# The first two weight blocks of an RWKV-5 and SwiGLU kernel, loaded and rounded by column halves

## The chip, the cores and the metric

The kernel runs on one core of one Trainium2 chip. The metric is the device time of one execution in microseconds (us); lower is better. A core has five engines that run programs of their own and meet at semaphores: TensorE (PE in the profile; its weight loads are PEld), VectorE (DVE), ScalarE (ACT), GpSimd (POOL) and SyncE (SP), which issues most of the DMAs. Sixteen DMA engines move what any of them issues.

## The reference

An RWKV-5 attention block with 4 batches, 8 heads, 768 steps and head size 48, in float32, feeds a SwiGLU feed-forward block of 3072 tokens, 384 channels and 1536 hidden channels:

```python
for t in range(S):
    kt, vt, rt = (k[:, :, t], v[:, :, t], r[:, :, t])
    cur = np.einsum('bhd,bhe->bhde', u[None] * kt, vt)
    y[:, :, t] = np.einsum('bhd,bhde->bhe', rt, state + cur)
    state = w[None, :, :, None] * state + np.einsum('bhd,bhe->bhde', kt, vt)
...
g = x @ w_gate
silu = g * (1.0 / (1.0 + np.exp(-g)))
val = x @ w_val
return (silu * val @ w_out).astype(np.float32)
```

Here x is y with its heads side by side, one row for each token. The three weight matrices arrive as float64 and r, k, v, w, u as float32.

## The kernel before

The attention is cut into 24 units of 128 steps; unit i is piece i // 4 of batch i % 4, up to unit 11. For one unit, `load(i)` fetches k and r (two DMAs on SP, rows of 48 floats), `load_v(i)` fetches v (two DMAs), `own_begin` and `own_end` form r*k*u on POOL, `own_sum` sums it on DVE, `diagonal` writes it into the tile At (ACT, and POOL for a part in the first units), `turn` transposes k and r on PE (line 405, eight matmuls, the four of k first) and DVE scales the results (line 407), `scores` multiplies them on PE (494) and DVE copies them under a mask into At (502), `outputs` multiplies At with v on PE (645) and ACT copies the result into xT (649), and `update` carries the state on (658). The raw k and r of units 0 to 3 are loaded into slots of the tile `hats`; r of unit 2 goes where r of unit 0 was.

The feed-forward block runs between these steps. `gate_value(g, f)` (line 688) multiplies 128 hidden columns f of w_gate and then of w_val with the x of units 2g and 2g+1, six float32 matmuls, each in two passes, so twelve in the profile; ACT applies Silu (694), DVE multiplies (695). `feed` takes such pieces out of a list at places that are fixed by hand.

The weights come as 64-bit floats, which no engine computes with, so they are rounded to float32 from their two 32-bit words. They are cut into 18 blocks (`chunks`); blocks 0 and 1 are the first 256 columns of w_gate and of w_val, 128 partitions times three rows of 256 doubles each. For a block, `load_weights` issues one DMA into a tile `bits` (three such tiles turn round; line 184), `round_high` turns the high words of one half into scaled magnitudes on ACT (204), `round_low` scales all the low words on ACT (210), `round_dve` puts sign and bits of one half into the weight tile on DVE (219 and 220), and `add_low` (228, one half) or `round_pool` (252, a whole block) adds the rounded low words on POOL. A half here is the first or the last 128 of the 256 columns, which are interleaved in the tile.

Every engine executes its instructions in the order in which the Python program issues them; nothing is reordered. On SP the order of the first loads is k and r of unit 0, k and r of unit 1, block 0, v of unit 0, block 1, v of unit 1, then k and r of unit 2, k and r of unit 3, block 2, v of units 2 and 3, block 3. On POOL, `own_begin(2)`, which reads k and r of unit 2, stands ahead of `add_low(0, 0)` and `add_low(1, 0)`; behind them come `own_end(2)`, `add_low(0, 1)`, `own_begin(3)`, `add_low(1, 1)`. The first `gate_value` needs `add_low(0, 0)` and, half way, `add_low(1, 0)`, and the x of units 0 and 1. The second needs the second halves. Between the two, PE transposes k and r of unit 3 and makes the scores of unit 2.

From unit 4 on the same steps run in a loop in which more blocks are rounded and more pieces fed; the later part multiplies by 3x3 schemes with fewer products (lines 957 and 1190) and projects with w_out (768).

Of the kernel before, what the change touches and what calls it, by code (L numbers as in the profile page):

```python
# [10 lines left out]
INT32 = mybir.dt.int32  # L11
UINT32 = mybir.dt.uint32
AF = mybir.ActivationFunctionType
ALU = mybir.AluOpType
AX = mybir.AxisListType
P = 128
# [6 lines left out]
def fast(  # L23
# [37 lines left out]
    two = ctx.enter_context(tc.tile_pool(name="two", bufs=2))  # L61
    three = ctx.enter_context(tc.tile_pool(name="three", bufs=3))
    ps_a = ctx.enter_context(tc.tile_pool(name="ps_a", bufs=1, space=bass.MemoryType.PSUM))
    ps_f = ctx.enter_context(tc.tile_pool(name="ps_f", bufs=1, space=bass.MemoryType.PSUM))
    dve, pool, act, pe, sp = nc.vector, nc.gpsimd, nc.scalar, nc.tensor, nc.sync
# [28 lines left out]
    def next_psum(m, n):  # L94
        t = ring_a[0]
        ring_a.rotate(-1)
        return t[:, 0 : m * n].rearrange("p (a x) -> p a x", a=m)
# [22 lines left out]
    def rhat_of(i):  # L120
        return rhat[i % 2 if i < BLOCKS else i % 4 // 2]

    def raw(i):

        if i < 4:
            return khat[i][:, :, 0:D], rhat[i % 2][:, :, 0:D]
        return k_ld[i % 2][:], r_ld[i % 2][:]
# [8 lines left out]
    def pieces_of(i):  # L136

        if i < PAIRED:
            c, b = divmod(i, B)
            return [(slice(0, P), b, P * c)]  # L140
        return [(slice(64 * p, 64 * p + 64), *part(i, p)) for p in range(2)]

    def load(i):
        for src, dst in zip((k, r), raw(i)):
            for rows, b, t in pieces_of(i):
                n = rows.stop - rows.start
                sp.dma_start(out=dst[rows], in_=src[b, :, t : t + n, :].rearrange("h t d -> t h d"))

    def load_v(i):
        for rows, b, t in pieces_of(i):  # L150
            n = rows.stop - rows.start
            for e in range(2):
                sp.dma_start(
                    out=v_ld[b][rows, :, 64 * e : 64 * e + D],
                    in_=v[b, :, t : t + n, :].rearrange("(a e) t d -> e t a d", e=2)[e],
                )


    chunks = []
# [9 lines left out]
    WN = 6 * P  # L169
    NW = len(chunks)  # L170
    bits, mags, lows = {}, {}, {}
    done = {"load": 0, "act": 0, "pool": 0}

    def next_chunk(stage):
        n = done[stage]
        done[stage] = min(n + 1, NW)
        return n if n < NW else None

    def load_weights():
        n = next_chunk("load")  # L180
        if n is not None:
            src = chunks[n][0].bitcast(INT32)
            bits[n] = three.tile([P, WN, 2], INT32, name="w_bits", tag="w_bits")
            sp.dma_start(
                out=bits[n][:].rearrange("p (c f) two -> p c (f two)", c=src.shape[1]), in_=src
            )
# [6 lines left out]
    def halves(x, n):  # L193

        c = chunks[n][1].shape[1]
        x = x.rearrange("p (c f) -> p c f", c=c)
        f = x.shape[2]
        return [x[:, :, 0 : f // 2], x[:, :, f // 2 : f]] if c == 3 else [x[:, 0:1], x[:, 1:2]]

    def round_high(n, half, bank):  # L200
        hi = halves(bits[n][:, :, 1], n)[half]
        mag = banks[2 + bank][:, 0 : WN // 2].bitcast(INT32)
        mags[n, half] = mag.rearrange("p (c f) -> p c f", c=hi.shape[1])
        act.activation(
            mags[n, half].bitcast(FP32), hi.bitcast(FP32), AF.Copy, scale=float(2.0**-112)
        )

    def round_low(n):
        lows[n] = two.tile([P, WN], INT32, name="w_low", tag="w_low")
        act.activation(  # L210
            lows[n][:], bits[n][:, :, 0].bitcast(UINT32), AF.Copy, scale=float(2.0**-29)
        )

    def round_dve(n, half):
        hi = mags.pop((n, half))
        f = hi.shape[2]
        dst = chunks[n][1].bitcast(INT32)
        dst = dst[:, :, half * f : half * f + f] if hi.shape[1] == 3 else dst[:, half : half + 1]
        dve.tensor_scalar(dst, hi, -(1 << 31), None, ALU.bitwise_and)
        dve.scalar_tensor_tensor(dst, hi, 3, dst, ALU.logical_shift_left, ALU.bitwise_or)  # L220

    def add_low(n, half):

        dst = chunks[n][1].bitcast(INT32)
        f = dst.shape[2] // 2
        cols = slice(half * f, half * f + f)
        low = lows[n][:].rearrange("p (c f) -> p c f", c=dst.shape[1])
        pool.tensor_tensor(dst[:, :, cols], dst[:, :, cols], low[:, :, cols], ALU.add)  # L228

    def round_first(n):  # L230
        round_high(n, 0, 0)
        round_low(n)
        round_dve(n, 0)

    def round_second(n):
        round_high(n, 1, 1)
        round_dve(n, 1)
        del bits[n]
        load_weights()
# [21 lines left out]
    def own_begin(i):  # L261
        kl, rl = raw(i)
        rks[i] = two.tile([P, H, D], FP32, name="rk", tag="rk")[:]
        pool.tensor_mul(rks[i], rl, kl)
# [8 lines left out]
    def own_sum(i):  # L273
        dus[i] = three.tile([P, H], FP32, name="du", tag="du")
        dve.tensor_reduce(dus[i][:], rks.pop(i), axis=AX.X, op=ALU.add)
# [12 lines left out]
    for e in range(2):  # L288
# [3 lines left out]
        out=u_row, in_=bass.AP(tensor=u.tensor, offset=u.offset, ap=[[0, 1], [1, H * D]]),  # L292
    )
    load(0)
    load(1)
    load_weights()
    load_v(0)
    load_weights()
    load_v(1)

    act.activation(sg0[:], ident[:, 0:1], AF.Silu)
    def warm(n, bank=None):
# [14 lines left out]
        out=mask[:, 0], in_=mask[:, 0], compare_op=ALU.is_gt, fill=0.0,  # L317
# [9 lines left out]
    for l in range(7):  # L327
        n = 1 << l
        f = pw[:, :, P - n : P - n + 1].to_broadcast([P, HP, n])
# [66 lines left out]
    def pair(t, a):  # L396
        return t[:, 2 * a : 2 * a + 2, :].rearrange("p e d -> p (e d)")

    def turn(i):
        kr = khat[i % 4], rhat_of(i)  # L400
        tps = [next_psum(HP, P) for _ in kr]
        turned[i] = three.tile([P, HP, P], FP32, name="rT", tag="rT")
        for tp, t, dst, table in zip(tps, kr, (kT[i % 2], turned[i]), (pw[:, :, 1 : P + 1], pv)):
            for a in range(HP):
                pe.transpose(tp[:, a, :], pair(t, a), ident[:])  # L405
            if i < 4:
                dve.tensor_mul(dst[:], tp[:], table)
            else:
                act.copy(dst[:], tp[:])
# [75 lines left out]
    def scores(i):  # L485

        ps = [next_psum(HP, P) for _ in range(2)]
        if i >= PAIRED:
            paired_scores(i, ps)
            return  # L490
        for a in range(HP):
            for e in range(2):
                rows = slice(64 * e, 64 * e + D)
                pe.matmul(  # L494
                    ps[e][:, a, :], kT[i % 2][rows, at(i, a), :], turned[i][rows, at(i, a), :],
                    start=True, stop=True, skip_group_check=True,
                )

        def masked_copy(e):
            dst = At[i % 2][:].rearrange("p (a e) t -> p a e t", e=2)[:, :, e]  # L500
            m = mask[:, 0].bitcast(INT32).unsqueeze(1).to_broadcast([P, HP, P])
            dve.copy_predicated(dst, m, ps[e][:])

        for e in range(2):
            lazy.append(lambda e=e: masked_copy(e))
        lazy.popleft()()
        if i < BLOCKS:
            lazy.popleft()()
# [854 lines left out]
    def flush():  # L1363
        while small:
            small.popleft()()
# [8 lines left out]
    diagonal(0)  # L1374
    flush()
    load(2)
    turn(1)
    own_sum(1)
    load(3)
# [4 lines left out]
    diagonal(1)  # L1384
    flush()
    round_high(0, 0, 0)
    round_low(0)
    round_high(1, 0, 1)
    round_low(1)
    scores(1)  # L1390
    round_dve(0, 0)
    own_begin(2)
# [11 lines left out]
    queue(0)  # L1404
    for n in range(2):
        round_high(n, 1, n)
        round_dve(n, 1)
        add_low(n, 1)
        del bits[n], lows[n]
        if n == 0:  # L1410
            own_sum(2)
            own_begin(3)
# [138 lines left out]
    n = nc.values_load(outside, min_val=0, max_val=512)  # L1551
# [6 lines left out]
@with_exitstack  # L1558
def kernel(
    ctx: ExitStack,  # L1560
    tc: tile.TileContext,
    *args: bass.AP,
):
    nc = tc.nc
    ctx.enter_context(tc.manual_schedule())
    flag = ctx.enter_context(tc.tile_pool(name="flag", bufs=1))
    outside = flag.tile([1, 1], INT32, name="outside")
    n = fast(tc, *args, outside[:])
    with tc.If(n > 0, label="general"):
        general(tc, *args)  # L1570
# [397 lines left out]
```

## Time and profile before

| | us |
|---|---|
| median of 3 runs | 581.36 |
| lowest and highest of them | 580.2 and 581.39 |
| the profiled execution, whole | 584.59 |
| its span, first to last instruction | 582.8 |
| busy in it: PE / DVE / POOL / ACT | 571.9 / 426.7 / 391.5 / 224.2 |

The profiled execution is one run of the program with the hardware profiler on; all rows below are from it, with times counted from the start of its span. The names in a row are the program's: "wgv<-wgv,w_low" writes tile wgv and reads wgv and w_low, "L228" is the line, "x2" the number of instructions, and what stands in brackets is the idle time before the group and what ended it. DMA rows on SP give the time of the issue, not that of the transfer.

### The profile page before, as it was taken

Reading aid. Unit: us, or ns where it says so; the run is one execution under the profiler, and the core shown is the slowest. Engines: PE = TensorE matmul, PEld = TensorE weight load, DVE = VectorE, ACT = ScalarE, POOL = GpSimd, SP = SyncE. Lnnn points to the kernel's source line nnn. Section 1 sums busy time; section 2 is a strip of 40 time slices with the busy share of each in tenths; the row PEclk is TensorE's granted clock in tenths of the full one; section 3 lists DMA queues with packets and bytes.
Section 4 is the critical chain, followed back from the end, with each engine's and each line's share of the span. In section 5 each row is a group of like instructions: output and inputs, shape, how many; then the busy total and the mean of one; then the engine's idle time right before and its main releaser. Section 6 shows DMA issues by size and latency. Waiting matters only on the chain.

```text
span 582.8 us, 13575 instructions
## 1 busy us (share of the span) xinstructions
PE 571.9 (98%) x5370; PEld 515.8 (89%) x5370; DVE 426.7 (73%) x745; ACT 224.2 (38%) x532; POOL 391.5 (67%) x395
## 2 busy tenths in 40 slices
PE   8899999999999999999999999999999999999996
PEld 7688888899988899988889988899988899988896
DVE  7677887488497789597869587869358877477672
ACT  3568878322354521344431343421143320233310
POOL 6589887999999737979536979527988950010610
PEclk9899999999999999999999999999999999999999
DMA  8978888562535425544324544220200000200002
GB/s 202 229 210 236 225 288 121 68 108 50 117 64 98 75 40 110 124 76 88 63 54 90 122 80 80 50 39 21 55 0 1 0 1 2 55 0 2 2 1 57
DMA packets 151734, 48.09 MB, mean 83 GB/s; under 512 B 139313, under 2 KB 142386, under 8 KB 151666
## 3 DMA queue, kind: packets, MB, share of 16 engines
q1 hardware_dynamic: 147218, 40.69, 33.9%
q10 hardware_dynamic: 4448, 6.49, 4.0%
q8 instruction: 43, 0.70, 0.5%
q14 instruction: 25, 0.20, 0.1%
HBM read 28.31 MB, written 4.72 MB: 57 GB/s over the span
## 4 chain that ended last, share of the span: by engine, by line
PE 97%; DMA 1%; issue 0%; DVE 0%; POOL 0%; ACT 0%; POOLq 0%
PE bank L957 32%; PE bank L768 19%; PE ring L957 13%; PE bank L688 12%; PE bank L1190 8%; PE ring L645 3%; PE ring L580 2%; PE ring L494 2%; PE ring L405 1%; PE ring L546 1%; PE ring L1190 1%; DMA hats<-in_r_dram 1%; PE ring L594 1%; PE ring L658 1%; PE ring L306 1%
## 5 line engine op out<-in xcount | busy, mean ns | idle before, releaser
L981 DVE TENSOR_TENSOR hv<-hv,bank 128x512 f32<-128x512 f32 x132 | 87.8, 682 | 38.5 <-PE bank L957 32.8
L688 PE MATMUL bank<-xT,wgv 128*128 128x256 f32 x288 | 68.3, 392 | 1.7 <-POOL wgv L228 1.5
L957 PE MATMUL bank<-xf,wgv 128*128 128x256 f32 x256 | 65.7, 381 | 0.0
L688 PEld LDWEIGHTS bank<-xT,wgv 128*128 128x128 f32 x288 | 54.3, 193 | 10.4 <-POOL wgv L228 1.7
L981 ACT COPY hv<-bank 128x512 f32<-128x512 f32 x72 | 40.8, 584 | 58.3 <-PE bank L957 52.7
L957 PEld LDWEIGHTS bank<-xf,wgv 128*128 128x128 f32 x256 | 48.0, 190 | 6.8 <-DVE kT L1235 0.6
L1244 POOL TENSOR_TENSOR hv<-At,hats 128x512 f32<-128x512 f32 x8 | 10.2, 1274 | 63.8 <-ACT At L1243 63.8
L988 ACT ACTIVATE hv<-hv 128x512 f32<-128x512 f32 (+2 forms) x36 | 22.7, 633 | 49.0 <-DVE hv L981 49.0
L376 ACT ACTIVATE zs<-mask,du 128x64 f32<-128x64 f32 x96 | 29.8, 346 | 20.4 <-DVE hv L781 9.3
L957 PE MATMUL bank<-xT,wgv 128*128 128x256 f32 x144 | 35.5, 379 | 0.0
L957 PE MATMUL bank<-xT,s 128*128 128x256 f32 x152 | 35.2, 380 | 0.0
L768 PE MATMUL bank<-wt,hs 128*128 128x192 f32 x192 | 34.1, 328 | 0.0
L768 PE MATMUL bank<-wo,hs 128*128 128x192 f32 x192 | 33.8, 326 | 0.0
L745 POOL TENSOR_TENSOR hs<-hv,hs 128x768 f32<-128x768 f32 x6 | 11.2, 1875 | 32.6 <-DVE hs L742 32.6
L768 PE MATMUL bank<-wo,hv 128*128 128x192 f32 x192 | 32.8, 327 | 0.0
L957 PEld LDWEIGHTS bank<-xT,s 128*128 128x128 f32 x152 | 28.7, 190 | 4.2 <-issue 0.2
L887 POOL TENSOR_TENSOR s<-s,wgv 128x256 f32<-128x256 f32 x39 | 30.1, 772 | 2.9
L768 PEld LDWEIGHTS bank<-wo,hv 128*128 128x128 f32 x192 | 31.6, 190 | 0.4
L887 POOL TENSOR_TENSOR s<-s 128x256 f32<-128x256 f32 x39 | 31.3, 802 | 0.9
L768 PEld LDWEIGHTS bank<-wo,hs 128*128 128x128 f32 x192 | 31.7, 190 | 0.2
L768 PEld LDWEIGHTS bank<-wt,hs 128*128 128x128 f32 x192 | 31.4, 190 | 0.2
L887 POOL TENSOR_TENSOR s<-wgv 128x256 f32<-128x256 f32 x39 | 29.6, 776 | 1.8 <-PE bank L768 1.8
(239 smaller groups left out, 1439.8 us busy)
## 6 DMA issues: line engine op xcount, KB each, us to landing
hats<-hats SPq DMA_DIRECT2D x96, 64.0 KB, 2.4
w_bits<-in_moe_w_gate_dram SPq DMA_DIRECT2D x6, 768.0 KB
w_bits<-in_moe_w_val_dram SPq DMA_DIRECT2D x6, 768.0 KB, 6.3
w_bits<-in_moe_w_out_dram SPq DMA_DIRECT2D x6, 768.0 KB, 7.0
At<-zs ACTq DMA_DIRECT2D x24, 128.0 KB, 3.7
At<-rT SPq DMA_DIRECT2D x24, 128.0 KB, 2.3
v_ld<-in_v_dram SPq DMA_DIRECT2D x24, 96.0 KB, 5.1
k_ld<-in_k_dram SPq DMA_DIRECT2D x24, 96.0 KB, 3.9
```

The source lines that it names most:

```text
L376: lambda h=h: act.activation(own[:, i % 2, slot(i, h), :], ident64, AF.Identity, scale=du[:, h : h + 1])
L494: pe.matmul(ps[e][:, a, :], kT[i % 2][rows, at(i, a), :], turned[i][rows, at(i, a), :], start=True, stop=True, skip_group_check=True,)
L580: pe.matmul(ps[32 * q : 32 * q + 32, cc, 64 * p : 64 * p + 64], *x, start=start, stop=stop, skip_group_check=True,)
L645: pe.matmul(ps[32 * q : 32 * q + 32, cc, :], *x, start=start, stop=stop, skip_group_check=True,)
L688: pe.matmul(gv[:, o, :].rearrange("p (i t) -> p i t", i=2), wt[:, c, P * f : P * (f + 1)], xT[:, 2 * g % NX : 2 * g % NX + 2, c, :], start ...
L745: on.tensor_sub(s[1], h12, x["s"][1])
L768: pe.matmul(ps, lhs[:, f, :], rhs[:, f, :], start=(f == 0 and n in (0, 1, 4)), stop=(f == FH - 1), skip_group_check=True,)
L887: op(made[o], made[a], made[b])
L957: pe.matmul(ps[:, o], u[:, o], v, start=first and o == 0, stop=True, skip_group_check=True,)
L981: do(out, *(pair_of(wide[a][:]) if isinstance(a, str) else a for a in args))
L988: todo.append((at, lambda: act.activation(gate, gate, AF.Silu)))
L1190: pe.matmul(ps, (h[what][q] if h[what] is D_ else h[what][:, q])[:, f, :], wide["o"][what][:, f, :], start=first and f == 0 and (split or ...
```

## The change

Blocks 0 and 1 are loaded by column halves. `load_half(n, half)` issues one DMA for 128 of the block's 256 columns; the first halves of both blocks are issued ahead of v of unit 0, where block 0 was, and the second halves behind k and r of unit 2, ahead of k and r of unit 3. `round_low` gets a half too: that of the first halves stays in its place, that of the second halves is done behind `round_high(n, 1, n)`. The later blocks are loaded and rounded whole, as before.

```diff
+    def load_half(n, half):
+
+        src = chunks[n][0].bitcast(INT32)
+        if half == 0:
+            bits[n] = three.tile([P, WN, 2], INT32, name="w_bits", tag="w_bits")
+            done["load"] = n + 1
+        c, f = src.shape[1], src.shape[2] // 2
+        sp.dma_start(
+            out=bits[n][:].rearrange("p (c f) two -> p c (f two)", c=c)[:, :, f * half : f * half + f],
+            in_=src[:, :, f * half : f * half + f],
+        )
+
...
-    def round_low(n):
-        lows[n] = two.tile([P, WN], INT32, name="w_low", tag="w_low")
-        act.activation(
-            lows[n][:], bits[n][:, :, 0].bitcast(UINT32), AF.Copy, scale=float(2.0**-29)
-        )
+    def round_low(n, half=None):
+        if not half:
+            lows[n] = two.tile([P, WN], INT32, name="w_low", tag="w_low")
+        out, x = lows[n][:], bits[n][:, :, 0]
+        if half is not None:
+            out, x = halves(out, n)[half], halves(x, n)[half]
+        act.activation(out, x.bitcast(UINT32), AF.Copy, scale=float(2.0**-29))
...
     load(0)
     load(1)
-    load_weights()
+    load_half(0, 0)
+    load_half(1, 0)
     load_v(0)
-    load_weights()
     load_v(1)
...
     diagonal(0)
     flush()
     load(2)
+    load_half(0, 1)
+    load_half(1, 1)
     turn(1)
     own_sum(1)
     load(3)
...
     round_high(0, 0, 0)
-    round_low(0)
+    round_low(0, 0)
     round_high(1, 0, 1)
-    round_low(1)
+    round_low(1, 0)
     scores(1)
...
     for n in range(2):
         round_high(n, 1, n)
+        round_low(n, 1)
         round_dve(n, 1)
         add_low(n, 1)
```

## The prediction

> **What bounds the kernel now.** I read the page first, then the chain of waits, then the engines' timelines around the one place where TensorE (PE) stands still, then tables by stretch of time.
>
> ```profile
> span 582.8 us, 13575 instructions
> ...
> PE 97%; DMA 1%; issue 0%; DVE 0%; POOL 0%; ACT 0%; POOLq 0%
> ```
>
> The last row is the chain that ended last: it is PE for 97% of the span, and one DMA for 1%. So a change can win only where PE waits or runs slowly. The chain in order of time (start, length, what) shows where the DMA stands in it:
>
> ```profile
> 12.04 6.19 DMA hats<-in_r_dram
> ...
> 19.33 1.01 POOL wgv L228
> ...
> 20.39 4.54 PE bank L688 x12
> ...
> 26.90 2.79 PE bank L688 x12
> ```
>
> Read it backwards. The first matmuls of gate_value (L688) start at 20.39, behind GpSimd's (POOL's) add of low words into the weights (L228). That add stands on POOL behind the product r*k of unit 2 (L264, `own_begin(2)`), which starts when r of unit 2 has landed, at 12.04 + 6.19 = 18.23. The add itself does not need r; it only stands behind it in program order. SyncE (SP) shows what stands ahead of that load in the DMA queue:
>
> ```profile
> 5.03 1.05 SPq L184 DMA_DIRECT2D w_bits<-in_moe_w_gate_dram  x1
> ...
> 7.21 0.51 SPq L184 DMA_DIRECT2D w_bits<-in_moe_w_val_dram  x1
> 7.76 3.59 SPq L153 DMA_DIRECT2D v_ld<-in_v_dram  x2
> 11.40 0.51 SPq L147 DMA_DIRECT2D hats<-in_k_dram  x1
> 12.04 2.25 SPq L147 DMA_DIRECT2D hats<-in_r_dram  x1
> ...
> 15.07 0.63 SPq L147 DMA_DIRECT2D hats<-in_r_dram  x1
> ```
>
> Two whole blocks of weights (L184; each is 128 x 3 rows of 256 doubles, 786.4 kB) go first, and loads of v between them; the last row is r of unit 3. The rates come from a table by stretch (start and end, length, busy time of PE, PEld, DVE, ACT and POOL, PE's granted clock, DMA share, GB/s):
>
> ```profile
> 16.00:18.00 2.00, 1.08 (x20) 0.65 (x12) 1.97 (x4) 2.00 (x5) 0.00 (x0) 1.00 1.02 194
> 20.00:21.00 1.00, 0.61 (x3) 0.56 (x4) 0.69 (x2) 0.00 (x0) 1.00 (x2) 1.00 1.00 383
> 21.30:24.70 3.40, 3.40 (x10) 2.62 (x9) 1.57 (x3) 0.00 (x0) 3.40 (x4) 0.50 1.05 245
> 60.00:582.80 522.80, 517.00 (x4749) 469.67 (x4747) 381.59 (x648) 188.08 (x445) 345.58 (x344) 1.00 0.33 67
> ```
>
> The same table for PE alone, over two stretches ahead of 21.3:
>
> ```profile
> 14.50:17.90 3.40, 2.47 (x60) 1.00 0.91 174
> 17.90:21.30 3.40, 1.57 (x8) 1.00 0.78 213
> ```
>
> Three things are to be seen. With k and r in the queues (rows of 48 floats, 192 bytes) full DMA engines move 194 GB/s; with weights (rows of 256 doubles, 2048 bytes) 383. PE's clock is 0.50 from 21.3 to 24.7, right behind a stretch of the same 3.4 us in which PE was busy for 1.57; behind a stretch with 2.47 it stayed at 1.00. And from 60 on PE is busy 517.0 of 522.8, so what is won before stays won.
>
> **The change part by part.** One: the queue ahead of r of unit 2. Before, two whole blocks, 2 x 786.4 kB at 383 = 4.11 us. After, two halves, together 786.4 kB in rows of 1024 bytes. No row shows that size. Its ends: at 383 it takes 2.05 (gain 2.05), at 194 it takes 4.05 (gain 0.06; rows longer than 192 bytes give no reason for less than that rate, so a loss here is left out). I put time per byte as a + b/size through the two rows, which gives 348 GB/s at 1024 bytes, an estimate near the upper row because the size is a factor of two from it and of five from the other: 2.26 us. Gain 4.11 - 2.26 = **1.85 us**: r lands at 16.38. SP issues as many transfers ahead of k and r as before (two), so nothing is added there. If the 2.25 us that SP spends in issuing r should shrink too, the gain is larger; its floor is in part three.
>
> Two: the halves that move behind r. They put two more issues (0.51 each by the row at 7.21) and 2.26 us of transfer ahead of k and r of unit 3; the queue ahead of those held 4.11 us of weights and now holds 4.52, so they come 0.41 later. The first half lands at 16.38 + 1.13 = 17.51, the second at 18.64. ScalarE (ACT) takes them here:
>
> ```profile
> 14.00 0.51 ACT L204 ACTIVATE bank<-w_bits 128x384 f32<-128x384 f32 x1
> 14.45 0.93 ACT L210 ACTIVATE w_low<-w_bits 128x768 int32<-128x768 uint32 x1
> 15.29 0.51 ACT L204 ACTIVATE bank<-w_bits 128x384 f32<-128x384 f32 x1
> ...
> 16.55 0.83 ACT L649 COPY xT<-ring 128x384 f32<-128x384 f32 x2
> ...
> 18.46 0.96 ACT L204 ACTIVATE bank<-w_bits 128x384 f32<-128x384 f32 x2
> 24.97 0.39 ACT L694 ACTIVATE sgs<-bank 128x256 f32<-128x256 f32 x1 [5.55 <-PE bank L688]
> ```
>
> A low-word pass of a whole block takes 0.84 from start to start, one of 384 columns 0.45. Twice 0.39 is saved near 14.5, twice 0.45 added near 19; the addition lies in the 5.55 us in which ACT waits for PE, so it costs nothing. Without that cover it would cost 0.90. The new waits on ACT (for 17.51 and 18.64) hold back nothing either, since ACT came there at 18.46 before and may be 0.78 sooner.
>
> Three: POOL and PE.
>
> ```profile
> 15.85 0.56 DVE L220 SCALAR_TENSOR_TENSOR wgv<-bank,wgv 128x384 int32<-128x384 int32 x1
> 18.36 1.01 POOL L264 TENSOR_TENSOR rk<-hats 128x384 f32<-128x384 f32 x1 [4.46 <-DMA hats<-in_r_dram]
> 19.33 1.96 POOL L228 TENSOR_TENSOR wgv<-wgv,w_low 128x384 int32<-128x384 int32 x2
> 23.15 1.01 POOL L264 TENSOR_TENSOR rk<-hats 128x384 f32<-128x384 f32 x1
> 24.11 1.01 POOL L228 TENSOR_TENSOR wgv<-wgv,w_low 128x384 int32<-128x384 int32 x1
> ```
>
> POOL idles 4.46 us ahead of r, so all of its row of work moves with r: product at 16.51, first add at 17.48, gate_value at 20.39 - 1.85 = 18.54. The floor is VectorE (DVE): the first add needs its result of 15.85 + 0.56 = 16.41, so gate_value cannot start before 16.45 + 1.05 = 17.50. That is the largest gain, 2.9.
>
> Four: the clock.
>
> ```profile
> 16.43 0.66 PE L405 MATMUL ring<-ident,hats 128*128 128x128 f32 x4
> 18.28 0.66 PE L405 MATMUL ring<-ident,hats 128*128 128x128 f32 x4 [1.19 <-DMA hats<-in_r_dram]
> 20.39 4.54 PE L688 MATMUL bank<-xT,wgv 128*128 128x256 f32 x12 [1.45 <-POOL wgv L228]
> 26.83 2.86 PE L688 MATMUL bank<-xT,wgv 128*128 128x256 f32 x12
> ```
>
> Twelve matmuls took 4.54 at the half clock and take 2.86 at the full one; the chain gives 2.79 for the later group, and 3.4 us at half speed lose 1.71. PE idles 1.19 and 1.45 around the second four transposes. After the change these follow the first four at once (r is there at 16.38, the first four end at 17.09) and end at 17.6; then 0.94 idle to 18.54. The emptiest 3.4 us of that hold 2.46 busy, as good as the 2.47 that kept the clock and far from the 1.57 that lost it. So **1.71 us** more.
>
> Next, what would be late. The second gate_value group moves from 26.83 to 23.27 and reads its value weights half a group (1.4) later, at 24.67. POOL's add for them moves from 24.11 to 22.26 and ends at 23.27: 1.4 to spare. For it the second half must land by 24.67 less 0.45 (ACT), 1.1 (DVE, two passes of 0.56) and 1.0 (POOL), that is by 22.1, 3.5 after my 18.64. One closer spot follows:
>
> ```profile
> 36.31 1.83 POOL L252 TENSOR_TENSOR wgv<-wgv,w_low 128x768 int32<-128x768 int32 x1 [1.57 <-ACT w_low L210]
> 40.13 1.83 POOL L252 TENSOR_TENSOR wgv<-wgv,w_low 128x768 int32<-128x768 int32 x1
> 41.80 2.76 PE L688 MATMUL bank<-xT,wgv 128*128 128x256 f32 x12
> ```
>
> The add that ends at 41.96 is needed at 41.80 + 1.4 = 43.2. Should POOL there follow r only (1.85) and PE 3.56, PE would wait 1.71 - 1.24 = 0.5. But POOL idles 1.57 ahead of the first of these, waiting for ACT, which follows PE; I cost it at nothing, 0.5 at most.
>
> The sum is 1.85 + 1.71 = 3.56. The profiled execution took 584.59 (span 582.8 and 1.8 around it), so it would take 581.03. The median of the three runs is 3.23 below that execution; from it, 581.36 - 3.56 = **577.8 us**.
>
> **The rivals.** B: only r's gain arrives. What turns the clock down depends on where the 3.4 us stretches begin; the runs of before reach from 580.2 to 581.39, which may be runs with and without the loss. If the median held no loss, or the changed kernel still has it, the time is 581.36 - 1.85 = 579.5. For it: one halving in one trace is thin evidence; against it: 0.94 idle is far less than 1.19 + 1.45. The Trainium skill, "TensorE: Matmul & The Clock Gate", Part 1, says that the clock halves after at least one idle window of about 3.4 us, and that the windows run free of the kernel's start. By its first half there was nothing here to halve the clock, as no idle stretch exceeds 1.45, and B would hold; this trace differs, since it shows 0.50. By its second half the loss may come and go between runs, which one trace can't show.
>
> C: a half block is as dear as a whole one. At the rate of the 192-byte rows the gain ahead of r is 0.06 and PE starts when it did. The four halves then take 8.1 us where the two blocks took 4.1, so r of unit 3 comes 4.0 later. The view of the tile that takes these loads gives their time from issue to landing:
>
> ```profile
> DMA to landing us min/median/max: 3.4/4.0/4.6
> ```
>
> Issued by 15.07 + 0.63, it landed by 20.3, and would land by 24.3: PE's transposes of it follow the first gate_value group, which ends at 24.9, so PE does not wait; POOL's product of 23.15 moves by 1.2, and the add behind it ends at 26.3, ahead of the 28.2 at which PE would read its result. Time 581.4, no change. For it: SP's 2.25 us in issuing r, during which the queue may be limited by something other than bytes. Against it: 194 and 383 differ by row size, and 1024 is nearer 2048. The Trainium skill, "DMA: Bandwidth & Descriptors", section Bandwidth, speaks against the change: it asks for 1 MiB per DMA and gives 32% of peak at 64 KB, 78% at 1 MB; the trace agrees only that small pieces are slower.
>
> D, slower: the passes over first halves wait for the whole tile, so that ACT's pass of 14.00 waits until 17.51 and that of 15.29 for the second half. Behind them on ACT stand the copies of x that gate_value reads. With the second half at 18.64, ACT does 2 x 0.45, then the two copies in 0.83, and gate_value starts at 20.4, as before: that is the point from which it decides. If the halves lag as much as r's issue stalled (2.25), it starts at 22.6: 581.36 + 2.2 = 583.6. Against it: interleaved halves of the weight tile are kept apart already, as DVE writes the second half while POOL adds into the first:
>
> ```profile
> 19.58 0.55 DVE L219 TENSOR_SCALAR wgv<-bank 128x384 int32<-128x384 int32 x1
> ```
>
> **How the numbers follow.** A, both gains, 0.55: 577.8, own range 576.7 (2.93 + 1.71) to 579.0 (r's gain only 0.65). B 0.26: 579.5. C 0.12: 581.4. D 0.07: 583.6. A and B hold 0.81; B's upper end, with a gain of 0.8, is 580.6, so the range is 576.7 to 580.6. About 0.2%, 1.2 us, is what a measurement of this kernel can tell from no change. Faster 0.81, the same 0.12, slower 0.07.
>
> **What would show it.** In the changed profile r of unit 2 lands near 16.4, POOL's L264 starts near 16.5, the first L688 group near 18.5 and takes 2.8 to 2.9 with the clock at 1.00; the second starts near 23.3 with no wait for POOL. Wrong would be: r near 18.2 (C), ACT's first L204 at 17.5 (D), a 0.50 stretch still there (B), or a wait of the second L688 group or of the transposes of unit 3, which the landing of the second halves or of r of unit 3 would end.

## The result, and the profile after

The changed kernel takes 584.18 us (median; 583.62 to 585.45), the kernel before 580.75 on the same chip. The ratio is 1.006, with an interval of 1.0047 to 1.0073: it is slower, by 3.4 us. On a second chip it was 582.99 against 580.96, ratio 1.0031 (1.0016 to 1.0047). The forecast was 577.8.

The profiled execution of the changed kernel took 583.8. Its first line, and its chain of waits by engine:

```profile
span 582.1 us, 13576 instructions
...
PE 95%; SPq 2%; DMA 1%; ACT 0%; issue 0%; DVE 0%; DVEq 0%; ACTq 0%
```

The chain in order of time (start, length, what) no longer passes through r of unit 2, but through a load of weights:

```profile
11.35 5.01 DMA w_bits<-in_moe_w_gate_dram
...
16.38 0.54 ACT bank L216
...
18.41 0.74 ACT xT L663 x2
19.15 0.39 ACT scales L379
...
19.67 4.51 PE bank L702 x12
```

L216 is `round_high`, which was L204; L702 is gate_value, which was L688. Which load is it that ACT waits for? SP's timeline has two of this block:

```profile
5.15 0.76 SPq L186 DMA_DIRECT2D w_bits<-in_moe_w_gate_dram  x1
...
10.66 0.65 SPq L147 DMA_DIRECT2D hats<-in_r_dram  x1
11.35 0.75 SPq L186 DMA_DIRECT2D w_bits<-in_moe_w_gate_dram  x1
```

The one of 11.35 is the second half, issued behind r of unit 2. But the pass that waits is the first one of ACT over block 0, which reads the first half alone. That half is not late: in e2_after below, the same program, the view of the tile gives 4.4 and 4.8 us from issue to landing for the two first halves, issued at 5.48 and 6.23, so both had landed by 11.1. The second half of block 0 landed there at 11.62 + 4.3 = 15.92, and ACT's first pass started at 15.96. The engines' timelines show how the wait is handed on (in brackets the idle time and what ended it):

```profile
16.38 0.53 ACT L216 ACTIVATE bank<-w_bits 128x384 f32<-128x384 f32 x1 [2.59 <-DMA w_bits<-in_moe_w_gate_dram]
...
19.04 0.87 ACT L379 COPY scales<-bank 128x384 f32<-128x384 f32 x2
16.94 0.56 DVE L233 TENSOR_SCALAR wgv<-bank 128x384 int32<-128x384 int32 x1 [1.94 <-ACT bank L216]
15.36 1.00 POOL L278 TENSOR_TENSOR rk<-hats 128x384 f32<-128x384 f32 x1 [1.77 <-DMA hats<-in_r_dram]
18.23 2.06 POOL L242 TENSOR_TENSOR wgv<-wgv,w_low 128x384 int32<-128x384 int32 x2 [1.88 <-DVE wgv L234]
16.05 1.09 PE L419 MATMUL ring<-ident,hats 128*128 128x128 f32 x8
19.67 4.51 PE L702 MATMUL bank<-xT,wgv 128*128 128x256 f32 x12 [2.53 <-ACT scales L379]
26.08 2.86 PE L702 MATMUL bank<-xT,wgv 128*128 128x256 f32 x12
```

r of unit 2 did come early: POOL takes it at 15.36, not at 18.36. But POOL, DVE and PE then stand idle for 1.88, 1.94 and 2.53 us, all behind ACT's 2.59. PE waits longest, because ACT's copies of the tables (L379) stand behind those passes and the copies of x, and gate_value writes into the bank that the first of them empties. The first group then takes 4.51 instead of 2.86. PE's table for the two stretches (length, PE busy, granted clock, DMA share, GB/s) says why:

```profile
17.06:20.47 3.41, 0.88 (x5) 1.00 0.95 242
20.47:23.88 3.41, 3.41 (x10) 0.50 0.97 191
```

Behind a stretch of 3.41 us in which PE was busy for 0.88, the clock is at half for as long.

One thing does not fit yet. The profiled execution of before had its second gate_value group at 26.83, this one at 26.08, so by the two profiles the change gains 0.75. By the medians it loses 3.4. The first experiment is for that.

### The profile page after: what moved, and what is told of

Read it like the earlier page. It is cut to its first block, busy times and chain, and to the rows that moved or that the text cites. A ratio compares the mean times of both kernels' runs of the same rounds, so it can differ in the third digit from the quotient of the medians.

```text
span 582.1 us, 13576 instructions
## 1 busy us (share of the span) xinstructions
PE 571.3 (98%) x5370; PEld 515.4 (89%) x5370; DVE 426.5 (73%) x745; ACT 224.6 (39%) x534; POOL 392.1 (67%) x395
## 4 chain that ended last, share of the span: by engine, by line
PE 95%; SPq 2%; DMA 1%; ACT 0%; issue 0%; DVE 0%; DVEq 0%; ACTq 0%
PE bank L971 32%; PE bank L782 19%; PE ring L971 13%; PE bank L702 12%; PE bank L1204 8%; PE ring L659 3%; PE ring L594 2%; PE ring L508 2%; PE ring L560 1%; PE ring L1204 1%; PE ring L419 1%; PE ring L608 1%; DMA w_bits<-in_moe_w_gate_dram 1%; SPq L147 1%; PE ring L672 1%; SPq L153 0%
## 5 line engine op out<-in xcount | busy, mean ns | idle before, releaser
L702 PE MATMUL bank<-xT,wgv 128*128 128x256 f32 x288 | 68.3, 392 | 2.8 <-ACT scales L379 2.5
L702 PEld LDWEIGHTS bank<-xT,wgv 128*128 128x128 f32 x288 | 54.4, 194 | 11.5 <-POOL wgv L242 2.7
```

The source lines that it names most:

```text
L702: pe.matmul(gv[:, o, :].rearrange("p (i t) -> p i t", i=2), wt[:, c, P * f : P * (f + 1)], xT[:, 2 * g % NX : 2 * g % NX + 2, c, :], start ...
```

## The experiments

All ran beside the kernel before, whose median was 580.96 beside e1 to e4 and 581.04 beside e5 to e8.

**e1_before: the kernel before once more, unchanged.** 

> The kernel of before, unchanged, timed against itself. The profiled execution of before took 584.59 us while its other runs took 580.2 to 581.4, so its profile may not show what those runs do. Theory 1 (the half-clock stretch comes and goes): its runs have a mean granted clock of 0.998 to 0.999 and spans near 579, without the stretch at half clock that the profile of before shows, and its new profile, if it is of such a run, shows the first gate_value group near 20.4 taking 2.8 instead of 4.5 us. Rival (the profile is only taken with an overhead): all runs have a clock of 0.996 and the new profile takes 584 to 585 with the half-clock stretch.

Measured: 580.78 (ratio 0.9995, 0.9978 to 1.0011). Theory 1 holds for the clock; the group's start, put near 20.4, came out sooner as well. Its profiled execution took 580.48, close to the median, where the one that the prediction was made from had taken 584.59. Its first line and timelines:

```profile
span 578.8 us, 13575 instructions
13.07 0.51 ACT L204 ACTIVATE bank<-w_bits 128x384 f32<-128x384 f32 x1
16.06 1.01 POOL L264 TENSOR_TENSOR rk<-hats 128x384 f32<-128x384 f32 x1 [3.09 <-DVE wgv L219]
17.02 1.97 POOL L228 TENSOR_TENSOR wgv<-wgv,w_low 128x384 int32<-128x384 int32 x2
15.70 1.09 PE L405 MATMUL ring<-ident,hats 128*128 128x128 f32 x8
18.08 2.86 PE L688 MATMUL bank<-xT,wgv 128*128 128x256 f32 x12 [1.28 <-ACT bank L204]
22.83 2.86 PE L688 MATMUL bank<-xT,wgv 128*128 128x256 f32 x12
```

(The page puts POOL's wait at 16.06 down to DVE; in the profiles of before, after and e3_packed the same instruction waits for r, and it reads nothing that DVE's passes write.) (PE's wait at 18.08 is put down to ACT's L204, a pass over a second half; gate_value doesn't need it, since in e5_product_later the group starts at 17.77 and that pass only at 18.28. What ends here at about 18.0 is the first of POOL's two adds of 17.02.) The same program starts POOL's product 2.30 earlier than in the first profile (18.36), at 16.06, the first group at 18.08 instead of 20.39, and there is no half clock: 2.86 instead of 4.54. The second group comes at 22.83 instead of 26.83, 4.00 earlier, and that is the whole difference of the spans (582.8 - 578.8). So the first profile was of an execution that is slow in just the place of the change. Such a one is rare: of 82 runs of the kernel before or copies of it (12 of e1_before, and 35 beside each four of the experiments), 8 had a mean granted clock of 0.996 or less, as the execution of the first profile had, and these took 582.85 to 584.75.

**e2_after: the changed kernel once more, unchanged.** 

> The changed kernel, unchanged, to have its runs beside those of before on one chip. Theory 1: every run has at least one half-clock stretch (clock 0.993 to 0.996), time 583.6 to 585.5. Rival (chance of the chip): it comes out within 0.2% of before here.

Measured: 582.99 (1.0031, 1.0016 to 1.0047). In 7 of its 12 runs the mean clock was 0.996 or less, not in all, as was expected. The profiled one, at 581.7, is one without the half clock:

```profile
span 580.0 us, 13576 instructions
15.96 0.54 ACT L216 ACTIVATE bank<-w_bits 128x384 f32<-128x384 f32 x1 [1.83 <-DMA w_bits<-in_moe_w_gate_dram]
19.33 2.83 PE L702 MATMUL bank<-xT,wgv 128*128 128x256 f32 x12 [1.70 <-ACT scales L379]
24.05 2.86 PE L702 MATMUL bank<-xT,wgv 128*128 128x256 f32 x12
```

Even so it starts the first group 1.25 later than e1_before (19.33 - 18.08) and its span is 1.2 longer. The other profile of the changed kernel adds the clock: its second group at 26.08 is 3.25 behind e1_before, 1.59 of it by the later start (19.67) and 1.66 by the half clock; its span is 3.3 longer. From the second group's start to the end the four profiles so far have the same time: 582.8 - 26.83 = 555.97 in the first profile of before, and 556.0, 555.97 and 555.95 in those of after, e1_before and e2_after. In these four, every microsecond is won or lost ahead of that group.

**e3_packed: the halves lie one behind the other in the tile.** The loads, their order and the passes are those of the changed kernel; only where the words of blocks 0 and 1 lie in `bits` differs:

```diff
+    def packed(t, half):
+        return t[:, WN // 2 * half : WN // 2 * half + WN // 2]
...
-            out=bits[n][:].rearrange("p (c f) two -> p c (f two)", c=c)[:, :, f * half : f * half + f],
+            out=packed(bits[n], half).rearrange("p (c f) two -> p c (f two)", c=c),
...
-        hi = halves(bits[n][:, :, 1], n)[half]
+        if n < 2:
+            hi = packed(bits[n], half)[:, :, 1].rearrange("p (c f) -> p c f", c=3)
```

and likewise in `round_low`. 

> The changed kernel with the two halves of blocks 0 and 1 packed one behind the other in their tile instead of interleaved, so that no range of one lies inside the range of the other; loads, order and passes as in the changed kernel. Theory 2 (the passes over first halves wait for the second halves because the wait is placed on the whole interleaved range): ACT's first pass starts near 13.8 us instead of 16.38, the first gate_value group near 17.5 (bounded by DVE's result at 16.1 to 16.4) instead of 19.67, PE idles under 1 us there, keeps its full clock, and the kernel takes 577 to 578.5. Rival (the loads themselves are what is slow): ACT's first pass still starts after 15 us and the time stays within 1 us of the changed kernel's.

Measured: 579.53 (579.08 to 580.48), ratio 0.9974 (0.996 to 0.9988). It beats both kernels, but misses the 577 to 578.5 expected. That time didn't fit its own start: by the other profiles (4.75 from group to group without the half clock, 555.97 behind, some 1.7 around the span) a group at 17.5 means 579.9. Its timelines:

```profile
span 577.4 us, 13578 instructions
13.16 0.52 ACT L223 ACTIVATE bank<-w_bits 128x384 f32<-128x384 f32 x1
14.55 1.02 POOL L286 TENSOR_TENSOR rk<-hats 128x384 f32<-128x384 f32 x1 [1.49 <-DMA hats<-in_r_dram]
15.65 2.06 POOL L250 TENSOR_TENSOR wgv<-wgv,w_low 128x384 int32<-128x384 int32 x2
15.53 1.09 PE L427 MATMUL ring<-ident,hats 128*128 128x128 f32 x8
16.71 2.86 PE L710 MATMUL bank<-xT,wgv 128*128 128x256 f32 x12
21.46 2.86 PE L710 MATMUL bank<-xT,wgv 128*128 128x256 f32 x12
```

ACT's first pass (L223) starts at 13.16 with no wait. r is taken at 14.55, 1.51 sooner than in e1_before, the group starts 1.37 sooner, right behind the transposes, and the span is 1.4 shorter. PE is busy for 3.28 of the 3.40 us from 14.50 to 17.90, so hardly anything more is to be had at this place, from an earlier k or r either.

**e6_packed_wait: e3_packed with the wait put back.**

```diff
+    for n in range(2):
+        act.copy(sg0[:], packed(bits[n], 1)[:, 0:1, 1].bitcast(FP32))
+        round_high(n, 0, n)
+        round_low(n, 0)
-    round_high(0, 0, 0)
-    round_low(0, 0)
-    round_high(1, 0, 1)
-    round_low(1, 0)
```

> The packed kernel (e3_packed, 579.53, first gate_value group at 16.71) with one thing put back: ahead of its first pass over each first half, ACT copies one column of the second half of the same block, so that it has to wait for the load of the second half as in the changed kernel. The layout of the tile, the loads and their order stay as in e3_packed. Theory (the changed kernel loses by this wait): ACT's first pass starts near 15.8 instead of 13.16, the copies of x and of the tables follow near 18 to 19, the first gate_value group starts near 19.2 instead of 16.71, as in the changed kernel (19.33), and the time is 582 to 583. Rival (the packed layout gains because its loads or passes are quicker, not because of the wait): the group starts by 17.2, the time stays below 580.

Measured: 583.11, ratio 1.0026 (1.0009 to 1.0042): the loss of the changed kernel is back, with its half clock (0.996 or less in 9 of 12 runs).

```profile
15.99 0.19 ACT L1411 COPY sg<-w_bits 128x1 f32<-128x1 f32 x1 [2.78 <-DMA w_bits<-in_moe_w_gate_dram]
16.09 0.52 ACT L223 ACTIVATE bank<-w_bits 128x384 f32<-128x384 f32 x1
19.44 4.45 PE L710 MATMUL bank<-xT,wgv 128*128 128x256 f32 x12 [2.87 <-ACT scales L387]
25.78 2.86 PE L710 MATMUL bank<-xT,wgv 128*128 128x256 f32 x12
```

e3_packed and e6_packed_wait differ in this wait and two copies of 0.19. So it is the wait, not quicker loads into the packed layout.

**e4_after_busy: the changed kernel with PE kept busy in the hole.** The four transposes of r of unit 2 are made six times instead of once:

```diff
-            for a in range(HP):
+            again = 6 if i == 2 and t is kr[1] else 1
+            for a in [*range(HP)] * again:
```

> The changed kernel in which PE repeats the four transposes of r of unit 2 five times more (20 matmuls, about 2.2 us) in the gap ahead of the first gate_value group; the results are the same. Theory 3 (the idle gap of 2.5 us costs the clock): the half-clock stretch behind the gap is gone, the first gate_value group takes 2.8 us instead of 4.5 and the kernel is 1.7 us or more faster than the changed kernel (582.5 or less). Rival (the gap costs only itself): the time stays at 584, or grows by up to 0.5 because the repeats delay DVE's scaling of r.

Measured: 582.24 (581.93 to 583.19), ratio 1.0021 (1.0007 to 1.0035), with the clock at 0.998 or more in all 12 runs.

```profile
15.61 3.27 PE L420 MATMUL ring<-ident,hats 128*128 128x128 f32 x28
19.23 2.83 PE L703 MATMUL bank<-xT,wgv 128*128 128x256 f32 x12 [0.35 <-ACT scales L379]
23.95 2.86 PE L703 MATMUL bank<-xT,wgv 128*128 128x256 f32 x12
```

With twenty matmuls that do nothing useful the median is 0.75 below that of e2_after (the intervals of the two ratios overlap). The expectation had 1.7 or more, against 584; but five of the twelve runs of e2_after have no half clock to lose. The start of the group (19.23) is nearly that of e2_after (19.33); only the half clock has gone. So the loss has two parts: the later start, which this edit leaves, and the clock, which it takes away.

**e7_low_halves and e5_product_later: the kernel before without moved loads.** e7_low_halves makes the low words by halves and nothing else. e5_product_later does that too, and puts POOL's product behind the adds:

```diff
-    own_begin(2)
     add_low(0, 0)
     outputs(0)
     round_dve(1, 0)
     add_low(1, 0)
+    own_begin(2)
     own_end(2)
```

> The kernel before with one part of the change alone: the low words are made by column halves (the second half behind the high words' second half), the loads are whole and in their old places. Theory: ACT is 0.8 us sooner with the copies of x and of the tables, but the first gate_value group is held by POOL (its product waits for r of unit 2), so it starts near 18.05 as before and the time is 580.8, no change. Rival (the half passes are what the packed kernel gains by): the group starts near 17, time 579.6.

> The kernel before with its whole-block loads in their old places. Two edits: on POOL the product r*k of unit 2 (own_begin(2)) stands behind the first adds of low words (add_low(0, 0), add_low(1, 0)) instead of ahead of them, and the low words are made by column halves. Theory (the first gate_value group of the kernel before is held by POOL's queue, not by the loads of weights as such): the first add starts when DVE has ended its two passes, near 15.5 instead of 17.0, PE's eight transposes of unit 2 end near 16.8, and the first gate_value group starts at 16.8 to 17.3 instead of 18.08 in the typical run of the kernel before: 0.8 to 1.3 us, so 579.5 to 580.0 against 580.8, without any load being moved. Rival (what matters is when r of unit 2 lands, by way of PE's transposes, and POOL's order is no limit): 580.8, no change.

Measured: e7_low_halves 580.86, ratio 0.9994 (0.9979 to 1.0008); e5_product_later 580.41, 0.9983 (0.9969 to 0.9996). POOL and PE of the first, then SP, ACT, POOL and PE of the second:

```profile
16.45 1.01 POOL L266 TENSOR_TENSOR rk<-hats 128x384 f32<-128x384 f32 x1 [2.92 <-DVE wgv L221]
18.48 2.86 PE L690 MATMUL bank<-xT,wgv 128*128 128x256 f32 x12 [1.27 <-POOL wgv L230]
```

```profile
12.47 2.23 SPq L147 DMA_DIRECT2D hats<-in_r_dram  x1
...
14.92 0.52 ACT L204 ACTIVATE bank<-w_bits 128x384 f32<-128x384 f32 x1 [0.48 <-DMA w_bits<-in_moe_w_val_dram]
15.90 2.06 POOL L230 TENSOR_TENSOR wgv<-wgv,w_low 128x384 int32<-128x384 int32 x2 [2.58 <-DVE wgv L222]
16.63 1.30 PE L407 MATMUL ring<-ident,hats 128*128 128x128 f32 x8
17.77 2.80 PE L690 MATMUL bank<-xT,wgv 128*128 128x256 f32 x12
...
22.46 2.86 PE L690 MATMUL bank<-xT,wgv 128*128 128x256 f32 x12
```

The half passes alone bring nothing, as expected. With the product out of the way the group starts without idle time, but at 17.77: now the transposes of unit 2 (16.63) are last. The gain of 0.6 is about half of the 0.8 to 1.3 expected. POOL's order held the typical kernel before by some tenths, an effect whose interval only just leaves out no change. This profiled execution took 580.86, 0.45 above its median, and its loads are late: SP issues r of unit 2 at 12.47, where it was 11.11 in e1_before, and ACT waits 0.48 for block 1. From its second group to the end it takes 579.1 - 22.46 = 556.64, 0.67 more than e1_before. How much of the miss comes from these, one profile can't say.

**e8_packed_ahead: e3_packed with all four halves ahead of k and r of unit 2.**

```diff
     load_half(0, 0)
-    load_half(1, 0)
+    load_half(0, 1)
     load_v(0)
+    load_half(1, 0)
+    load_half(1, 1)
...
-    load_half(0, 1)
-    load_half(1, 1)
```

> The packed kernel (e3_packed) with all four half blocks ahead of k and r of unit 2: the second half of each block is queued right behind its first half, in the places of the whole blocks of the kernel before. Passes and layout stay as in e3_packed. Theory (the gain of e3_packed is r of unit 2 landing 1.5 us sooner): r lands at 16.0 or up to 0.5 later, as four half loads stand ahead of it, POOL's product starts near 16.1 to 16.6, the first gate_value group at 18.1 to 18.6, time 580.8 to 581.3, no gain over the kernel before. Rival (the gain of e3_packed is in the half passes or the layout): group near 16.7 to 17, time 579.6.

Measured: 580.81, ratio 0.9991 (0.9973 to 1.0009).

```profile
16.27 1.00 POOL L286 TENSOR_TENSOR rk<-hats 128x384 f32<-128x384 f32 x1 [2.13 <-DMA hats<-in_r_dram]
18.29 2.86 PE L712 MATMUL bank<-xT,wgv 128*128 128x256 f32 x12 [0.46 <-POOL wgv L250]
```

Packed halves without the earlier r gain nothing. So what e3_packed gains is the order of the loads, the idea of the change itself.

## Why the prediction was wrong

**The step that failed first: "The new waits on ACT (for 17.51 and 18.64) hold back nothing either, since ACT came there at 18.46 before ..."** The wait for the second half of block 0 does not stand at the second pass, but at the first: 16.38 instead of 13.07 in e1_before. That is rival D, which had 0.07. Its point of decision was worked out nearly right: it put the group at 20.4, and it came to 19.67 with the second half of block 0 at 16.36 (11.35 + 5.01), 1.15 sooner than the 17.51 forecast. But that was compared with the 20.39 of the first profile, not with 18.08, so D looked harmless where it costs 1.25 to 1.6. D also left the copies of the tables (L379) out of ACT's queue; the chain shows that gate_value waits for the first of them, which ends at 19.15 + 0.39, and starts 0.13 later. With that, D's sum holds in e2_after: the second half of block 1 landed at 12.34 + 4.7 = 17.04 by the view of the tile, and 17.04 + 0.90 + 0.83 + 0.39 + 0.13 = 19.29, where the group started at 19.33.

**The argument against D** was DVE's row of 19.58: DVE writes the second half of `wgv` while POOL adds into the first. That shows it for that tile and those two forms of access only. The loads into `bits` and the passes that read every other word of it were not kept apart, though they touch different words. That the packed layout takes the wait away and one copied column brings it back is shown; why the interleaved pieces are taken as one is not.

**The base of the sum.** Both gains, 1.85 for r and 1.71 for the clock, were counted on the path of the profiled execution, where r was taken at 18.36 and the clock was halved behind the wait. It stood 3.23 above the median, and the two gains add up to 3.56: the prediction wrote down both numbers and subtracted the second from the median. In e1_before r is taken at 16.06 and the clock is not halved, so nothing of the 1.71 was there to win. r itself came 1.51 sooner in e3_packed than in e1_before, of which PE could use 1.37. Rival B's premise, that the median held no clock loss, was right, and its price of 1.85 for r too high. That its 579.5 is nearly e3_packed's 579.53 is luck: the base of 581.36, from three runs, was 0.40 above the 580.96 measured beside e3_packed. Even without the wait the time would thus have been about 579.5, in the range, and not 577.8. (Two small slips decide nothing: from the floor at 17.50 the largest gain is 2.89, not 2.93, and 3.4 us at half speed lose 1.70.)

**Step one, the bytes ahead of r, was right.** The rate of half blocks was put at 348 GB/s. In the changed kernel the table by stretch has 369 just ahead of the landing of the second half of block 0 (16.36), near the 383 of the whole blocks:

```profile
14.50:16.00 1.50, 1.32 (x44) 0.90 (x34) 0.50 (x1) 0.00 (x0) 0.64 (x1) 1.00 1.09 369
```

So rival C is out. The Trainium skill, "DMA: Bandwidth & Descriptors", section Bandwidth, asks for 1 MiB per transfer; halving 786.4 kB cost 4% of the rate here, as far as that stretch holds half blocks alone. r was taken at 15.36 and 14.55, sooner than the 16.38 forecast for its landing, for the base was too late as well.

**Step four, the clock, had the right mechanism and the wrong sign.** An empty stretch in front of gate_value does bring the half clock: 0.88 busy of 3.41 did here, 2.88 of 3.20 in e4_after_busy did not. The change was to close that hole, and the wait on ACT made it wider, so the typical run now has a loss that it did not have. The Trainium skill, "TensorE: Matmul & The Clock Gate", Part 1, speaks of an idle window of some 3.4 us; the longest idle time was 2.53 here and 1.45 in the first profile, and the clock was halved, so by these traces a stretch of that length that is idle for more than half is enough (busy 0.88 of 3.41 here, 1.57 of 3.40 in the first profile). That the windows run free of the kernel agrees with runs of one program with and without the loss, as in e2_after.

**What came next was right.** The second group never waits for POOL (2.86 each time), the later k and r of unit 3 hold nothing, and the tight spot at block 3 costs nothing: from the second group on, e3_packed too has 555.94 (577.4 - 21.46). Of the other edited kernels e7_low_halves agrees (555.97); e8_packed_ahead with 556.15, e4_after_busy with 556.35, e5_product_later with 556.64 and e6_packed_wait with 555.42 stand off by up to 0.7. Why was not followed.

## What to carry to other kernels

Before a gain is read from a trace, compare the profiled execution's own time with the median: where it stands as far above as the gain that you find, the trace may show a loss that the median doesn't have. When a load is split into halves so that the first can be used early, look in the trace at which of the two loads ends the wait of the first reader, and lay the halves out as separate ranges. A wait put into an engine's queue costs what stands behind it: here copies that had nothing to do with the weights, and through the hole in PE's work its clock.

## What the runs showed of the hardware

One program differs from run to run in when a load lands: POOL took r of unit 2 at 18.36 in one execution of the kernel before and at 16.06 in another, 2.3 us apart. SP issued it at 12.04 there; in e1_before SP's timeline has

```profile
11.11 2.36 SPq L147 DMA_DIRECT2D hats<-in_r_dram  x1
```

so 0.93 of the difference lies ahead of the issue. From issue to landing it took at most 16.06 - 11.11 = 4.95, since POOL reads it then, where it had taken 6.19. (The view of the tile gives no landing for this load in either execution; the 3.4 to 4.6 that the prediction took from it are those of other loads.) What delays it was not tried and stays open. Whether a hole in PE's work halves the clock also changes from run to run: a hole of 1.70 in e2_after did not, 2.53 in the same program did. Useless matmuls in the hole did not delay the group (19.23 against 19.33) and kept the clock (0.998 or more in all 12 runs).
